# Fused strided attention and MoE on one core: new rules and a new order in the list scheduler, the softmax term as a column, gates kept in PSUM

## The chip, the core and the metric

The kernel runs on one core of a Trainium2 chip as one launch. The metric is the device time of the launch in microseconds; lower is better. The kernel before has a median of 315.19 us over three runs (315.13 to 317.72).

## The reference, cut to what matters

Attention over 8 batches, 8 heads, 576 positions and head size 64 in f32. Heads 0 to 3 see the last 32 positions, heads 4 to 7 every 32nd position. Its output, as 4608 rows of 512, goes to a mixture of 8 experts that picks one expert per row and keeps at most 80 rows of each expert, those with the greatest gate.

```python
mask_local = (rel >= 0) & (rel < stride)
mask_strided = (rel >= 0) & (pos[None, :] % stride == pos[:, None] % stride)
scores = scores - np.max(scores, axis=-1, keepdims=True)
attn = np.exp(scores)
attn = attn / (np.sum(attn, axis=-1, keepdims=True) + 1e-09)
...
probs = np.exp(logits_shift)
probs /= probs.sum(-1, keepdims=True) + 1e-09
gate_w = probs[np.arange(N), expert_idx]
...
keep = np.argpartition(-gw, capacity)[:capacity]
h = np.maximum(x[tok_idx] @ w1[e], 0.0)
out[tok_idx] = gate_w[tok_idx, None] * (h @ w2[e])
```

## The kernel before, in words

The program has three stages.

**Attention**, up to about 213 us of the profiled execution. It is cut into 32 steps j = 4b + 2g + it: batch b, kind of mask g (0 local, 1 strided), half it. For each step PE writes a mask and the scores into PSUM banks (`do_scores`, L503 to L531); DVE takes the maximum (L537) and the difference into an SBUF tile `pb` (L539); ACT makes the exponential in place (L546); DVE sums rows of 64 or 18 (L549), adds 1e-9 (L550) and inverts (L551) into `sm`; POOL multiplies `pb` by `sm` (L553). Two steps later `do_values` transposes `pb` on PE (L581, L612), ACT or DVE copies the result to SBUF, and PE multiplies with v (L598, L641) into `xt`. `do_logits` computes the gate logits of a batch on PE (L657, L660), turns them (L665), and a chain of small DVE instructions (L668 to L699, with an exponential on ACT, L685) makes `gates`. `do_rows` turns `xt` into rows on PE (L732), copies them to an SBUF buffer `xn` (L353, L357) and stores them to `xs` in DRAM (L741). Besides this, POOL moves `vlo` (L461) and `cp` (L411), and 20 chunks of expert weights of 512 KB are loaded (L270) and split into two f16 halves: the high half on POOL or ACT (L280, L278), the low half on DVE (L774).

The order of attention is not written by hand. Each piece of work is an `Op` given to `Plan.add` with a priority, the engine or engines it may run on, a cost in us and what it reads and writes. `Plan.order` is a greedy list scheduler: it advances a clock per engine, picks the earliest operation within `SLACK`, breaks ties by a priority with a random part (`SEED`, `SPREAD`), chooses between ACT and DVE for an operation marked "AV", hands out the 8 PSUM banks, and fills idle PE time with matmuls that nobody reads (`filler`, L370), up to planned time `FILL0` and again past priority `FILL1`. The result is the program order of every engine's queue, SP's included, which issues all loads and stores; each engine runs its queue in that order. Operations marked `lag` (the weight splits) that the plan starts after the last gates go to `late_ops`, and zero fills of `out` that didn't fit go to `pl.dropped`; both are issued after the rows (after L999).

**Router**, about 213 to 241 us. DVE picks 16 candidates per lane (L985 to L998), PE spreads them (`call`, L996), POOL builds `val` (L1019 to L1030), DVE ranks them (L1037 to L1061), PE sums the kept (L1064, L1065), DVE makes one-hot tables (L1075), PE multiplies them (L1078), DVE makes the row numbers `idx` (L1087), and POOL gathers rows (L1092). Rows that the plan doesn't place (`RN` = 14 of the 24 half blocks of the last 4 batches are in it) are turned, copied and stored here by ACT (`rows_left`), through the four buffers of `xns2`, which lie in `vlo` and `ktl`. `warm(n)` (L319) lets PE run n matmuls that nobody reads: 48 behind the rows, 32 behind L1078.

The tiles of the router lie in a pool `rt` that is opened when the pools of attention (`ap`, `am`, `al`) have been closed. It uses their memory, so the first writer of a router tile waits for the last user of the attention tile that lay there.

**Experts**, about 241 to 310 us. 16 halves (w1 or w2 of an expert). PE runs the matmuls (L1149 to L1151, L1171, L1173) while ACT and DVE split the weights of later halves (`wsplit`: L278, L288) and SP reloads the chunk buffers, 8 of them; `xe` is the gathered block of rows turned and split (L1141, L1143, L1144).

## Time and profile before

| | us |
|---|---|
| median of 3 runs | 315.19 |
| profiled execution | 315.96 |
| its span | 314.2 |
| outside the span (315.96 - 314.2) | 1.8 |
| PE busy of the span | 268.0 |
| DVE busy | 244.9 |
| ACT busy | 227.7 |
| POOL busy | 147.4 |
| moved by DMA | 84.24 MB |

Busy times of engines overlap, so they don't add up to the span. Matmuls are pipelined and the profiler draws one until its result is written, so PE's busy time is more than the time it takes from the span. In rows of the trace the first number is the start in us from the span's start, the second how long the engine was in that group; "x12" counts instructions; a bracket at the end gives the idle time ahead of the group and what ended it. "issue" means that the profile shows nothing that the engine waited for.

### The profile page before, as it was taken

The page shows a single profiled execution, that of the slowest core. Times are in us where ns is not written, and L with a number is a line of the kernel's source. Part 1 is how long each engine was busy: PE and PEld are TensorE (multiplying, and loading weights), DVE is VectorE, ACT ScalarE, POOL GpSimd, SP SyncE. Part 2 cuts the span into 40 slices and gives each one's busy share as a digit, 9 for nine tenths or more (in the row PEclk, how much of TensorE's full clock was granted, in tenths as well). Part 3 has the DMA queues.
Part 4 walks back from the last instruction along what each step waited for, and adds up shares of the span by engine and source line. Part 5 has one row for each costly group of instructions (what it writes and reads, how often), then busy time and mean ns, then how long its engine had stood idle before and what let it go on. Part 6 is the DMA issues. An engine that isn't in the chain of part 4 may idle for free. (4 is left out here: it accounts for less than half of the span.)

```text
span 314.2 us, 12290 instructions
## 1 busy us (share of the span) xinstructions
PE 268.0 (85%) x5144; PEld 235.9 (75%) x5144; DVE 244.9 (78%) x489; ACT 227.7 (72%) x446; POOL 147.4 (47%) x170
## 2 busy tenths in 40 slices
PE   7996999899886999889599889896654989999991
PEld 7975977688765987768587758665653989999991
DVE  7594689899997499996778888754484899999980
ACT  1765767789697798779577885775612888999961
POOL 8646458437463556467418518403126252333432
PEclk9999899999999899999799988998955999999997
DMA  8899999999999599997399999869889999999901
GB/s 256 163 269 384 226 265 265 279 293 289 292 287 232 182 261 259 335 277 223 108 249 237 281 246 281 286 170 300 253 266 309 335 371 382 400 385 383 365 28 48
DMA packets 49373, 84.24 MB, mean 268 GB/s; under 512 B 23201, under 2 KB 23201, under 8 KB 49314
## 3 DMA queue, kind: packets, MB, share of 16 engines
q1 hardware_dynamic: 48290, 80.79, 87.4%
q0 software_dynamic: 1024, 2.62, 2.6%
q8 instruction: 42, 0.69, 0.9%
q14 instruction: 17, 0.14, 0.2%
HBM read 63.21 MB, written 20.19 MB: 265 GB/s over the span
## 5 line engine op out<-in xcount | busy, mean ns | idle before, releaser
L553 POOL TENSOR_TENSOR pb<-pb,sm 128x288 f32<-128x288 f32 (+2 forms) x32 | 34.8, 1090 | 66.8 <-DVE sm L551 39.1
L461 POOL TENSOR_SCALAR vlo<-vlo 32x1152 f32<-32x1152 f32 (+1 forms) x32 | 37.8, 1181 | 7.2 <-ACT qt L355 1.8
L774 DVE SCALAR_TENSOR_TENSOR spl<-ring,spl 128x1024 f16<-128x1024 f32 x20 | 27.8, 1398 | 9.3 <-ACT spl L278 9.3
L598 PE MATMUL bank<-ptl,vlo 128*64 128x64 f32 x576 | 24.0, 236 | 9.3 <-issue 8.8
L1149 PE MATMUL hp<-xe,spl 128*128 128x80 f16 x256 | 30.8, 205 | 0.6 <-ACT xe L1143 0.6
L1150 PE MATMUL hp<-xe,spl 128*128 128x80 f16 x256 | 30.7, 205 | 0.7 <-issue 0.3
L1151 PE MATMUL hp<-xe,spl 128*128 128x80 f16 x256 | 30.7, 205 | 0.4 <-issue 0.4
L353 ACT COPY ktl<-bank 64x384 f32<-64x384 f32 (+1 forms) x49 | 26.4, 566 | 5.8 <-DMA xs<-ktl 2.6
L598 PEld LDWEIGHTS bank<-ptl,vlo 128*64 128x64 f32 x576 | 20.8, 147 | 12.7 <-issue 10.8
L1171 PE MATMUL yp<-he,spl 128*128 128x160 f16 x256 | 28.4, 233 | 0.9 <-DVE he L1166 0.9
L1173 PE MATMUL yp<-he,spl 128*128 128x80 f16 x256 | 28.0, 199 | 0.4 <-issue 0.4
L549 DVE TENSOR_REDUCE sm<-pb 128x16 f32<-128x288 f32 (+2 forms) x32 | 22.7, 710 | 7.0 <-ACT pb L546 6.9
L353 ACT COPY ptl<-bank 64x256 f32<-64x256 f32 (+2 forms) x46 | 21.3, 473 | 9.4 <-PE bank L581 5.0
L546 ACT ACTIVATE pb<-pb 128x288 f32<-128x288 f32 (+2 forms) x32 | 18.1, 565 | 13.7 <-DVE pb L539 13.4
L278 ACT ACTIVATE spl<-ring 128x1024 f16<-128x1024 f32 x23 | 23.8, 1059 | 5.7 <-DMA ring<-moe_w 5.7
L288 DVE SCALAR_TENSOR_TENSOR spl<-raw,spl 128x1024 f16<-128x1024 f32 x21 | 26.6, 1288 | 1.0 <-ACT spl L278 1.0
L1150 PEld LDWEIGHTS <-spl 128*128 128x128 f16 x256 | 26.1, 102 | 1.3 <-issue 1.2
L1151 PEld LDWEIGHTS <-spl 128*128 128x128 f16 x256 | 26.1, 102 | 0.9 <-issue 0.9
L1149 PEld LDWEIGHTS <-spl 128*128 128x128 f16 x256 | 26.2, 102 | 0.0
L1173 PEld LDWEIGHTS <-spl 128*128 128x128 f16 x256 | 25.0, 98 | 1.4 <-issue 1.4
L1171 PEld LDWEIGHTS <-spl 128*128 128x128 f16 x256 | 25.1, 98 | 0.9 <-issue 0.9
L628 ACT ACTIVATE pts<-bank,hm 72x288 f32<-72x288 f32 x52 | 21.9, 494 | 3.8 <-DVE pts L622 2.0
(212 smaller groups left out, 776.9 us busy)
## 6 DMA issues: line engine op xcount, KB each, us to landing
ring<-moe_w SPq DMA_DIRECT2D x32, 512.0 KB
raw<-moe_w SPq DMA_DIRECT2D x21, 512.0 KB
raw<-q SPq DMA_DIRECT2D x16, 576.0 KB
out<-kst SPq DMA_DIRECT2D x9, 1024.0 KB
raw<-k SPq DMA_DIRECT2D x15, 576.0 KB
kst<-moe_w SPq DMA_DIRECT2D x11, 512.0 KB
xs<-xn SPq DMA_DIRECT2D x12, 384.0 KB
vs<-v SPq DMA_DIRECT2D x8, 512.0 KB
```

What stands on the lines that cost most here:

```text
L278: nc.scalar.activation(hi, r, AF.Copy, scale=SC)
L288: nc.vector.scalar_tensor_tensor(lo, r, SC, hi, op0=ALU.mult, op1=ALU.subtract)
L353: nc.scalar.copy(o, i)
L461: add(4 * b + m + 0.6 + 0.4 * u, "P", 1.25 if m == 0 else 1.1, lambda e: nc.gpsimd.tensor_scalar(vlo[64 * u:64 * u + 32, t0:t1], vlo[64 * ...
L553: add(pj(j) + E_MUL, "P", 0.2 + 1.7e-3 * nt * nk, lambda e: nc.gpsimd.tensor_tensor(plain(pa, g), plain(pa, g), spread(sm[:, 0:nt], g), op ...
L598: nc.tensor.matmul(o[64 * h:64 * h + 64, :, k0:k0 + 32], vlo[:, 2 * (t0 + c0 + c) + p, h], ptl[:, c0 + c, :, 32 * gg:32 * gg + 32], start= ...
L774: add(pr + 0.2, "V", 1.14, lambda e: nc.vector.scalar_tensor_tensor(lo, r, SC, hi, op0=ALU.mult, op1=ALU.subtract), rd=nm + [("hi", i)], l ...
L1149: nc.tensor.matmul(o, w[:, 0, i:i + P], x[:, 0, c], start=first, stop=False)
L1150: nc.tensor.matmul(o, w[:, 0, i:i + P], x[:, 1, c], start=False, stop=False)
L1151: nc.tensor.matmul(o, w[:, 1, i:i + P], x[:, 0, c], start=False, stop=last)
L1171: nc.tensor.matmul(o.rearrange("p a s -> p (a s)"), w[:, 0, i:i + P], x.rearrange("p a s -> p (a s)"), start=first, stop=False)
L1173: nc.tensor.matmul(o[:, 0], w[:, 1, i:i + P], x[:, 0], start=False, stop=last)
```

## The change

What it does, part by part:

1. **The planner** gets two rules. Operations of DVE and POOL that are marked `port` aren't started while the other engine runs one that is marked too. PE instructions are counted (`ni`), and behind every `NIB` = 252 of them the next can't start before `FETCH` = 5.5 us have passed since the block of instructions before it was entered. Numbers are changed with it: seed, `PEN`, `DLAT`, `E_EXP`, `E_SUM`, `E_O`, `W0`, `LASTN`, `XP0`, `XPS`.
2. **1e-9 as a column**: `pb` becomes wider, with a column of 1e-9 beside every row of 64 (or 18) weights, written once at the start. The sum reads it along with the weights, so the instruction of L550 falls away; in the gates `gex` has a ninth column, and L697 falls away.
3. **Gates**: `lg` and `eq` are no SBUF tiles any more, but columns of the PSUM bank that held the turned logits.
4. **The rows**: `RN` 20 instead of 14 of the last 24 half blocks are in the plan; three of the rest (`XL`) stand ahead of `call`; seven buffers in turn (`xns`, one in `qt`, four as before) instead of four.
5. **The router**: `late_ops` are issued behind the first gather, no longer ahead of the ranking; the one split that stood there goes; 3 splits (`RS`) instead of 1 stand behind the flag, ahead of the first `xe`, and 2 (`NS0`) behind it, as before. `warm` is 48 matmuls behind L1078 in the old numbering, and none behind the rows.
6. The first copies of q and k into `cp` may run on ACT too.

```diff
-    def add(self, prio, eng, cost, fn, rd=(), wr=(), mode=None, take=(), size=0, bg=False, after=(), lag=False, drop=False):
+    def add(self, prio, eng, cost, fn, rd=(), wr=(), mode=None, take=(), size=0, bg=False, after=(), lag=False, drop=False, ni=0, port=False):
...
+                    if o.port:
+                        a, z = port["P" if e == "V" else "V"]
+                        if e in port and a <= t < z:
+                            t = z
...
+            if e == "T":
+                left = NIB - count
+                count += o.ni
+                if count >= NIB and o.ni:
+
+                    x = t + c * left / o.ni
+                    c += max(0.0, entered + FETCH - x)
+                    entered, count = max(x, entered + FETCH), count - NIB
+            if o.port and e in port:
+                port[e] = (t, t + c)
...
+    gex = const.tile([NQ, NC6, E + 1], F32, name="gex")
...
-    pbs = [ap.tile([P, (640, 512, 288, 288)[i]], F32, name=f"pb{i}") for i in range(NPB)]
+    pbs = [ap.tile([P, (650, 520, 304, 304)[i]], F32, name=f"pb{i}") for i in range(NPB)]
...
             for j in range(3):
-                add(l - 2.5, "V", 0.53, lambda e, j=3 * j: nc.vector.tensor_copy(o[:, j:j + 3], i[:, j:j + 3]),
-                    rd=[raw_(l % 3)], wr=[CPS[w][j]])
+                add(l - 2.5, "AV", dict(A=0.45, V=0.53), lambda e, j=3 * j: copy(e, o[:, j:j + 3], i[:, j:j + 3]),
+                    rd=[raw_(l % 3)], wr=[CPS[w][j]], port=True)
...
+    def with_term(pb, g, n):
+        return pb[:, 0:65 * n].rearrange("p (t c) -> p t c", c=65) if g == 0 else \
+            pb.rearrange("p (t c z) -> p t z c", c=19, z=4)
...
         def total(e):
             nc.vector.tensor_reduce(each(sm[:, 0:nt], g), pq, op=ALU.add, axis=AX.X)
-            nc.vector.tensor_scalar(sm[:, 0:nt], sm[:, 0:nt], 1e-9, None, op0=ALU.add)
             nc.vector.reciprocal(sm[:, 0:nt], sm[:, 0:nt])
...
-            nc.vector.tensor_reduce(sg, w["ex"], op=ALU.add, axis=AX.X)
-            nc.vector.tensor_scalar(sg, sg, 1e-9, None, op0=ALU.add)
+            nc.vector.tensor_reduce(sg, gex, op=ALU.add, axis=AX.X)
...
         def lsum(e):
-            w["lg"] = sp.tile([NQ, NC6, E], F32, name="lg")
+            for k_, nm in enumerate(("lg", "eq")):
+                w[nm] = cols(y, 512)[0:NQ, 384 + 64 * k_:432 + 64 * k_].rearrange("p (c e) -> p c e", e=E)
...
+        j = k_ % 2 if b < DEF else (k_ - 3 * DEF) % 7
+        if j < 2:
+            return xns[j], [("xn", j)]
+        return xns2[j - 2], [("xns2", j)] + [[("qt", a) for a in range(3)],
...
+    nc.vector.memset(gex, 1e-9)
+    for t in pbs:
+        nc.vector.memset(t, 1e-9)
...
-    for o in late_ops + pl.dropped:
+    for o in pl.dropped:
         o.fn(o.on)
...
     gather(0)
-    wsplit()
+    for o in late_ops:
+        o.fn(o.on)
     for e in range(1, NX):
         gather(e)
-    flush()
...
-    for _ in range(3 - RS):
+    for _ in range(NS0):
         wsplit()
...
-RN = 14
+RN = 20
 XR = 0
-XL = 4
+XL = 3
 WARM = 44
-WARM_ = [48, 0, 32, 0]
-RS = 1
+WARM_ = [0, 0, 48, 0]
+RS = 3
+NS0 = 2
...
-SEED, SPREAD = 99245, .3
+SEED, SPREAD = 71497, 0.3
...
-LASTB, LASTN = 3, 2
+LASTB, LASTN = 3, 3
...
+NIB, IC0, FETCH = 252, 126, 5.5
```

Three places where the queues differ. The first is DVE from the last gates to the ranking, with the semaphores that each row waits for (`g` is the turned gates, `cvi` or `cv` and `ci` the candidates, `pos` the first tile of the ranking). Before:

```order
L699 TENSOR_TENSOR gates<-eq,sg 96x48 [waits DVE_49]
L904 COPY g_116<-bank_150 128x96 [waits PE_49]
L985 MAX cvi<-g_116 128x8 [waits DVE_49]
L986 MATCH_REPLACE qs<-cvi,g_116 128x288 [waits DVE_49]
L987 MAX cvi<-qs 128x8 [waits DVE_49]
L990 TENSOR_TENSOR wgt<-cvi,segm 128x256 [waits DVE_49]
L997 MAX_INDEX cvi<-cvi,g_116 128x8
L998 MAX_INDEX cvi<-cvi,qs 128x8
L774 SCALAR_TENSOR_TENSOR spl_129<-ring_122,spl_129 128x1024 [waits DMAHW0_49,Activation_49]
L1037 TENSOR_SCALAR pos<-cvi 128x16 [waits DVE_49]
L1039 TENSOR_SCALAR scr,rank<-call,cvi 128x256 [waits PE_49]
```

Now:

```order
L737 TENSOR_TENSOR gates<-bank_152,sg 96x48 [waits DVE_49]
L944 COPY g_117<-bank_152 128x96 [waits PE_49]
L1026 MAX cv<-g_117 128x8 [waits DVE_49]
L1027 MATCH_REPLACE qs<-cv,g_117 128x288 [waits DVE_49]
L1028 MAX cv<-qs 128x8 [waits DVE_49]
L1031 TENSOR_TENSOR wgt<-cv,segm 128x256 [waits DVE_49]
L1038 MAX_INDEX ci<-cv,g_117 128x8
L1039 MAX_INDEX ci<-cv,qs 128x8
L1078 TENSOR_SCALAR pos<-cv 128x16 [waits DMAHW0_49,DMAHW1_49,DVE_49,Activation_49]
L1080 TENSOR_SCALAR scr,rank<-call,cv 128x256 [waits PE_49]
```

The split of a weight chunk (L774) between the candidates and the ranking is gone. `pos` now waits for an ACT copy and two stores as well: in the program these are the copy into the row buffer that lies in `qt` and the two stores from that buffer, because `pos` lies where `qt` lay. The first instruction of POOL's `pieces` waits for the same.

The second place is SP's queue from the first stores of the last rows to the first loads of the expert stage (`xs<-` are row stores, `out<-kst` are zero fills of 1 MB). Before, and below it now:

```order
L741 DMA xs<-ktl 96x1024
L741 DMA xs<-vlo 96x1024 x2
L741 DMA xs<-ktl 96x1024 x2
L270 DMA ring_122<-moe_w 128x1024
L794 DMA out<-kst 256x1x1024
L270 DMA kst<-moe_w 128x1024
L270 DMA kst<-moe_w 128x2x512
L270 DMA raw<-moe_w 128x2x512 x3
```

```order
L295 DMA ring_123<-moe_w 128x1024
L834 DMA out<-kst 256x1x1024 x2
L780 DMA xs<-vlo 96x1024
L295 DMA ring_124<-moe_w 128x1024
L780 DMA xs<-ktl 96x1024
L780 DMA xs<-xn_181 96x1024
L780 DMA xs<-xn_182 96x1024
L780 DMA xs<-qt 96x1024
L780 DMA xs<-vlo 96x1024
L780 DMA xs<-ktl 96x1024
L780 DMA xs<-vlo 96x1024 x2
L295 DMA raw<-moe_w 128x2x512 x3
```

All zero fills and weight loads of the plan now stand ahead of the last row stores, the last stores go to five buffers in turn instead of two, and the loads into `raw` are the first behind them, where a weight load and a zero fill were.

The third place is DVE from the flag to the first block of rows (`ovfb` is what PE multiplies to sum the flag, `fls` and `fli` the flag). Before, and below it now:

```order
L1114 CAST ovfb<-ovf 128x2
L1117 TENSOR_REDUCE fls<-small 1x1
L1119 CAST fli<-fls 1x1
L288 SCALAR_TENSOR_TENSOR spl_3610<-ring_122,spl_3610 128x1024
L1144 SCALAR_TENSOR_TENSOR xe<-xp,xe 128x320
L288 SCALAR_TENSOR_TENSOR spl_3610<-raw,spl_3610 128x1024
```

```order
L1155 CAST ovfb<-ovf 128x2
L1158 TENSOR_REDUCE fls<-small 1x1
L1160 CAST fli<-fls 1x1
L313 SCALAR_TENSOR_TENSOR spl_3424<-ring_123,spl_3424 128x1024
L313 SCALAR_TENSOR_TENSOR spl_3424<-ring_124,spl_3424 128x1024
L313 SCALAR_TENSOR_TENSOR spl_3424<-raw,spl_3424 128x1024
L1185 SCALAR_TENSOR_TENSOR xe<-xp,xe 128x320
```

Three splits now stand between the flag and the first block of rows (`xe`), where one stood; before, another one (of `ring_121`) stood some rows further up, right behind `idx` (L1087), and now none does.

More of the change, by code (lines that the diff above doesn't have):

```diff
@@ L92, in order @@
         dma, mode, fills = 0.0, None, []
+        port = dict(V=(0.0, 0.0), P=(0.0, 0.0))
+        count, entered = IC0, 0.0
         rng = random.Random(SEED)
@@ L137, in order @@
                     f.mode, f.cost, f.deps, f.take, f.size, f.lag = 128, m * C_FILL, [], (), 0, False
+                    f.port, f.ni = False, 2 * m
+                    count += f.ni
+                    if count >= NIB:
+                        entered, count = f.start, count % NIB
                     fills.append(f)
@@ L344, in moe_attention @@
     xns2 = [t[0:NQ, 1024 * j:1024 * j + 1024].rearrange("p (x f) -> p x f", x=2)
-            for t in (vlo.rearrange("p t h d -> p (t h d)"), ktl.rearrange("p h u s -> p (h u s)")) for j in range(2)]
+            for t, m in ((qtl.rearrange("p h s -> p (h s)"), 1), (vlo.rearrange("p t h d -> p (t h d)"), 2),
+                         (ktl.rearrange("p h u s -> p (h u s)"), 2)) for j in range(m)]
     def cols(x, n):
@@ L434, in do_transposes @@
             add(pr, "T", C_TR * 3, fill, rd=[CPS[w][j3]] if g == 0 else nm, wr=[x], take=[x], mode=128,
-                after=[((("qt", j3), ("qs", j3))[g]) if w == 0 else ((("ktl", u, j3), ("kst", u, j3))[g]) for u in range(len(dvs))])
+                after=[((("qt", j3), ("qs", j3))[g]) if w == 0 else ((("ktl", u, j3), ("kst", u, j3))[g]) for u in range(len(dvs))], ni=6)
             for u, d in enumerate(dvs):
@@ L462, in do_overlap @@
             vlo[64 * u:64 * u + 32, t0:t1], vlo[64 * u + 32:64 * u + 64, t0 - 1:t1 - 1], 1.0, 0.0,
-            op0=ALU.mult, op1=ALU.add), rd=[("vlo", u, m), ("vlo", u, 0)], wr=[("vlq", u, m)])
+            op0=ALU.mult, op1=ALU.add), rd=[("vlo", u, m), ("vlo", u, 0)], wr=[("vlq", u, m)], port=True)
     def rows_of(t, g):
@@ L510, in do_scores @@
                                                                          [("qs", a) for a in range(3)] + KST + ["mstr", "kstz"]),
-                wr=[x], take=[x], mode=128, after=[("p", j % NPB, bk)])
+                wr=[x], take=[x], mode=128, after=[("p", j % NPB, bk)], ni=4 if g == 0 and t == 0 else 2)
             if g == 0:
@@ L521, in mm @@
                                                  tile_position=(0, 32 * gg))
-                add(pj(j), "T", 0.112 * n, mm, rd=[("qt", a) for a in range(3)] + KTL + ["ktlz"], wr=[x], mode=32)
+                add(pj(j), "T", 0.112 * n, mm, rd=[("qt", a) for a in range(3)] + KTL + ["ktlz"], wr=[x], mode=32, ni=8 * n)
                 t += n // 2
@@ L532, in mm @@
                                                  start=False, stop=(rr == 1 and z == 3), tile_position=(0, 32 * h))
[L533 removed]
+                    add(pj(j), "T", 0.57, mm, rd=[("qs", a) for a in range(3)] + KST + ["kstz"], wr=[x], mode=32,
+                        ni=64)
             sv = lambda x=x, n=n: rows_of(cols(x, n * nk), g)
[L535 removed]
+            pv_ = by_row(weights(pb, g, o, n), g)
             su = lambda x=x, n=n: plain(cols(x, n * nk), g)
@@ L575, in do_values @@
             t0 = TL[it][0]
+            pn = [[("ptl", a, u) for a in ((a,) if it == 0 else (0, 1))] for a in range(2) for u in range(2)]
             for a, (c0, c1) in enumerate(TG[it]):
@@ L580, in fill @@
                     for c in range(n):
-                        nc.tensor.transpose(cols(x, 512)[:, P * c:P * c + P], pb[:, P * (c0 + c):P * (c0 + c) + P], ident)
+                        nc.tensor.transpose(cols(x, 512)[:, P * c:P * c + P], pb[:, 130 * (c0 + c) + 1:130 * (c0 + c) + 129], ident)
                 add(pj(j) + E_PT, "T", C_TR * n, fill, rd=PN, wr=[x], take=[x], mode=128,
-                    after=[("ptl", a, u) for u in range(2)])
+                    after=pn[2 * a] + pn[2 * a + 1], ni=2 * n)
                 for u in range(2):
@@ L599, in mm @@
                                                  ptl[:, c0 + c, :, 32 * gg:32 * gg + 32], start=True, stop=True)
-                add(pj(j) + 2, "T", 0.25 * n, mm, rd=[("ptl", a, u) for u in range(2)] + [("vlq", u, it) for u in range(2)] +
-                    [("vlo", u, it) for u in range(2)] + ["vloz"], wr=[x], take=[x], mode=64, after=nm)
+                add(pj(j) + 2, "T", 0.25 * n, mm, rd=pn[2 * a] + pn[2 * a + 1] + [("vlq", u, it) for u in range(2)] +
+                    [("vlo", u, it) for u in range(2)] + ["vloz"], wr=[x], take=[x], mode=64, after=nm, ni=16 * n)
                 add(pj(j) + 2 + E_O, "AV", c_copy(P * n), lambda e, x=x, c0=c0, c1=c1, n=n: copy(
@@ L611, in fill @@
                 for a in range(4):
-                    nc.tensor.transpose(t[0:72, a], pb[:, 72 * a:72 * a + 72], ident)
+                    nc.tensor.transpose(t[0:72, a], pb[:, 76 * a:76 * a + 72], ident)
             add(pj(j) + E_PT, "T", C_TR * 4, fill, rd=PN, wr=[x], take=[x], mode=128,
-                after=[("pts", z) for z in (0, 2)])
+                after=[("pts", z) for z in (0, 2)], ni=8)
             def tv(x):
@@ L755, in do_rows @@
         xn, nm = xn_of(b, hf)
-        add(pr, "T", C_TR * 4, lambda e: fill(cols(x, 512)), rd=xt_of(b, part)[1], wr=[x], take=[x], mode=128)
+        add(pr, "T", C_TR * 4, lambda e: fill(cols(x, 512)), rd=xt_of(b, part)[1], wr=[x], take=[x], mode=128, ni=8)
         add(pr + E_EV, "AV", c_copy(512), lambda e: ev(e, cols(x, 512), xn),
```

81 lines of the change are left out of this document (39 added, 42 removed).

## Prediction

> **What bounds the kernel now.** I read the slices of the span and the windows view first, to find which engine limits which stretch; then the waits of PE, since PE is busiest in the longest stretch; then the timelines of the stretch between.
>
> ```profile
> 8.00:213.00 205.00, 182.49 (x3585) 153.95 (x3582) 163.10 (x353) 157.56 (x340) 105.92 (x103) 0.97 0.94 255
> 245.00:306.00 61.00, 58.36 (x1278) 56.97 (x1275) 58.41 (x63) 55.66 (x84) 21.90 (x23) 1.00 0.91 334
> 102.10:152.40 50.30, 44.71 (x885) 37.96 (x885) 40.22 (x88) 40.38 (x88) 27.53 (x25) 0.97 0.89 255
> 101.60:104.90 3.30, 2.80 (x33) 2.68 (x34) 1.65 (x6) 1.20 (x3) 2.75 (x3) 0.50 0.87 286
> 152.80:156.10 3.30, 3.30 (x25) 3.18 (x21) 1.61 (x5) 1.98 (x4) 1.94 (x3) 0.50 0.11 25
> ```
>
> (After the window: its length, then busy us and count of PE, weight loads, DVE, ACT, POOL; last the granted clock, the DMA share and GB/s.) Attention is a PE stage: 182.49 of 205 us, DVE 163.10, with DMA close behind at a share of 0.94. The expert stage has PE and DVE level, 58.36 and 58.41 of 61.
>
> ```profile
> PE bank L598 <- issue: 8.8, 7, 3.2
> PE bank L612 <- POOL pb L553: 2.8, 3, 1.1
> PE bank L519 <- issue: 1.2, 1, 1.2
> PE bank L641 <- issue: 1.2, 1, 1.2
> PE bank L531 <- issue: 0.4, 2, 0.2
> PE bank L432 <- DVE pb L539: 0.6, 2, 0.4
> ```
>
> Of PE's waits in attention (total, times, longest) the largest ended on nothing that the profile shows: 8.8 + 1.2 + 1.2 + 0.4 = 11.6 us of "issue". For DVE it waits 0.6.
>
> ```profile
> 99.03 0.57 PE L598 MATMUL bank<-ptl,vlo 128*64 128x64 f32 x12
> 102.10 1.76 PE L598 MATMUL bank<-ptl,vlo 128*64 128x64 f32 x28 [2.50 <-issue]
> 152.45 0.89 PE L598 MATMUL bank<-ptl,vlo 128*64 128x64 f32 x15 [3.16 <-issue]
> q8 instruction: 42, 0.69, 0.9%
> ```
>
> Between the two stalls lie 885 = 7 x 126 + 3 matmuls, each of two PE instructions. So the stalls recur at a fixed count, 252 instructions, and a DMA queue brings the instructions (0.69 MB / 42 = 16 KB a packet). A block of short matmuls ends before its successor is there. Behind a stall of this length the granted clock is 0.50 for 3.30 us (two windows above).
>
> From the last copy of gates (`g`, which I call T0 = 212.76) to PE at full pace:
>
> ```profile
> 212.76 0.26 DVE L904 COPY g<-bank 128x96 f32<-128x96 f32 x1 [0.46 <-PE bank L791]
> 215.44 0.45 DVE L998 FIND_INDEX8 cvi<-cvi,qs 128x8 uint32<-128x288 f32 x1
> 224.26 1.23 DVE L774 SCALAR_TENSOR_TENSOR spl<-ring,spl 128x1024 f16<-128x1024 f32 x1 [8.37 <-ACT spl L278]
> 225.41 0.17 DVE L1037 TENSOR_SCALAR pos<-cvi 128x16 f32<-128x16 f32 x1
> 233.10 0.17 DVE L1087 TENSOR_REDUCE idx<-tab 80x8 int32<-80x16 f32 x1 [0.81 <-PE tab L1078]
> 236.61 0.15 DVE L1117 TENSOR_REDUCE fls<-small 1x1 f32<-1x2 f32 x1 [0.80 <-PE small L1115]
> 236.87 1.23 DVE L288 SCALAR_TENSOR_TENSOR spl<-ring,spl 128x1024 f16<-128x1024 f32 x1
> 239.94 0.77 PE L1141 MATMUL xp<-ident,xg 80*128 80x80 f32 x4 [3.37 <-DMA xg<-xs,idx]
> 241.81 0.23 PE L1150 MATMUL hp<-xe,spl 128*128 128x80 f16 x1 [0.30 <-DVE xe L1144]
> ```
>
> DVE stands 8.37 us before the ranking (`pos`), behind one split whose ACT half was late: ACT had row copies ahead of it, and those waited for stores from their buffers (the 2.63 in a row further down). The stretch is 241.81 - 212.76 = 29.05 us long.
>
> **The change part by part, in attention (what it does to T0).**
>
> *Instruction blocks.* I took the printed order of PE in both kernels, gave every matmul the mean spacing that its form has in the trace, and summed each 126. Before, the blocks fall short of 5.5 us by 10.9 in total, where the profile has 11.6: the model holds. The new order falls short by 5.4: -5.5. Ends: -7 (its short blocks stretched by waits) and 0 (the stalls don't follow this rule).
>
> *Half clock.* Each long stall costs about 3.3 x 0.5 = 1.7 us more. Summed in the same way, the shortest block before is 2.7 us and now 3.8, so stalls of 2.5 us and more shouldn't come again; I take one of the two as gone: -1.7 (-3.4 to 0).
>
> *Twenty more row transposes* (five half blocks of four) stand ahead of T0 in PE's order:
>
> ```profile
> 213.07 2.00 PE L732 MATMUL bank<-ident,cp 128*96 128x128 f32 x16 [0.35 <-DVE g L904]
> 210.59 1.50 PE L370 MATMUL bank<-identb 128*128 128x128 bf16 x24
> ```
>
> At 2.00/16 = 0.125 us that is +2.5. 75 fewer fillers (0.06 each, second row, 4.7 us) stand in the order, but they lie where PE would wait: 0, and -4.7 would be the end below.
>
> *The gates' tail.* In the chain that gives T0 there is now no split:
>
> ```profile
> 209.49 1.22 DVE L774 SCALAR_TENSOR_TENSOR spl<-ring,spl 128x1024 f16<-128x1024 f32 x1
> 210.62 0.20 DVE L688 TENSOR_TENSOR eq<-lg,m 96x48 f32<-96x48 f32 x1
> 211.68 0.17 DVE L697 TENSOR_SCALAR sg<-sg 96x6 f32<-96x6 f32 x1
> ```
>
> The split held L688 for 1.1, L697 took 0.2. Against that stand the PSUM operands of the gates: the copy of 96 columns from PSUM above took 0.26 where SBUF instructions of 48 take 0.20, so up to 0.06 for each of some six: -1.0 (-1.3 to -0.9).
>
> *The 1e-9 column.* It removes 32 + 8 instructions of DVE:
>
> ```profile
> L550 DVE TENSOR_SCALAR sm<-sm 128x16 f32<-128x16 f32 (+2 forms) x32 | 11.6, 364 | 1.1
> L697 DVE TENSOR_SCALAR sg<-sg 96x6 f32<-96x6 f32 x8 | 2.9, 362 | 0.3
> ```
>
> 14.5 us of DVE (364 ns is a mean over 171 to 1005). I value it at 0: PE's own work covers it, since PE waits 0.6 us for DVE in the whole stage; were that cover gone, the end below is -0.6. New at the start are memsets of 1778 columns on DVE, by the splits (1024 columns, 1.22 us) 1.6 to 2.1, partly under the first loads: +0.5 (0 to +1).
>
> *Port rule.* Reordered DVE and POOL work that PE doesn't wait for longer than 2.8 us: inside the terms above.
>
> *DMA.* Two row stores, a weight chunk and a zero fill more go out ahead of T0: 2 x 0.39 + 0.52 + 1.05 = 2.4 MB, at 255 GB/s 9.3 us. The idle share, 6% of 205 = 12.3 us, takes it nearly all: +1 (0 to +3).
>
> *Moved work.* The last weight split (1.2 us of DVE, about 1 us of ACT) and the zero fill that stood behind T0 stand ahead of it. DVE has 205 - 163.1 = 42 us without work there and ACT 47, and PE hardly waits for either: 0. The same holds for three early copies of `cp` that may go to ACT, which is idle then. What the split frees behind T0 is counted below.
>
> Sum: -5.5 - 1.7 + 2.5 - 1.0 + 0.5 + 1 = **-4.2**. The ends add up to -14.4 and +5.6, but they can't all come together, since stalls, fillers and waits share the same idle time of PE; I keep -9 to +3.
>
> A rule of the Trainium skill speaks against the first term: "Runtime: NRT & Kernel Launch", Instruction fetch mechanics, says that crossing a 16 KiB boundary costs one DMA tail-bump that is mostly hidden. The trace disagrees, with 11.6 us of issue stalls at that period. By the page the blocks would be worth nothing, nor would the half clock behind them, T0 would move by 2.5 - 1.0 + 0.5 = +2.0, and the first rival below would hold.
>
> **The stretch behind T0.** *Ranking.* The split is gone, and `pos` now waits for the row copy into `qt` and its store:
>
> ```profile
> 211.15 0.44 SPq L741 DMA_DIRECT2D xs<-ktl  x1
> 217.19 1.07 ACT L353 COPY ktl<-bank 96x512 f32<-96x512 f32 x2 [2.63 <-DMA xs<-ktl]
> 218.28 0.32 SPq L741 DMA_DIRECT2D xs<-ktl  x1
> 221.23 2.05 ACT L353 COPY ktl<-bank 96x512 f32<-96x512 f32 x4
> ```
>
> A store behind other transfers landed 217.19 - 211.15 = 6.0 us after issue, one in a thin queue 221.23 - 218.28 = 2.95 or less. The second `qt` copy stands about 1 us behind T0, so `pos` starts at T0 + 4.6; the ends are T0 + 3.1 (candidates done, 215.89) and T0 + 7.2. From `pos` to the end of `idx` took 233.27 - 225.41 = 7.86.
>
> ```profile
> 216.06 0.23 POOL L1019 CAST pieces<-cvi 128x16 bf16<-128x16 f32 x1 [15.63 <-DVE cvi L998]
> 219.91 1.28 POOL L1030 TENSOR_TENSOR val<-pieces,esel 128x640 bf16<-128x640 bf16 x1
> 231.61 1.46 PE L1078 MATMUL tab<-val,oh 128*80 128x40 bf16 x16 [1.19 <-DVE oh L1075]
> ```
>
> POOL's `val` takes 221.19 - 216.06 = 5.1 and runs beside the ranking now; L1078 needs it 231.61 - 225.41 = 6.2 behind `pos`, so it is hidden, with +0.3 (0 to 1.5) for two engines on one port. `idx`: T0 + 12.8 instead of T0 + 20.5.
>
> *Flag and splits.* 48 fillers stand ahead of the flag's matmul where 32 stood:
>
> ```profile
> 222.03 2.84 PE L319 MATMUL bank<-identb 128*128 128x128 bf16 x48
> 232.90 3.58 PE L319 MATMUL bank<-identb 128*128 128x128 bf16 x32
> ```
>
> At the pace of the second row 48 x 3.58/32 = 5.4 (by the first 2.8). They start 0.4 ahead of the end of `idx`: T0 + 17.8; flag to DVE 236.87 - 236.41 = 0.46: T0 + 18.3; three splits of 1.2: T0 + 21.8; L1144 to full PE pace 0.5: **T0 + 22.3**. The gather is next: issue 0.3 behind `idx`, landing 239.94 - 233.58 = 6.4, then 241.81 - 239.94 = 1.9: T0 + 21.4, a microsecond earlier. So 29.05 - 22.3 = **-6.7**; with `pos` at T0 + 7.2 and the contention -4.0, with the early `pos` and fast fillers -8.9.
>
> **Expert stage**: the same instructions on two level engines, 0; the loads have one chunk less, so a gain of up to 1.2 isn't excluded.
>
> **Sum**: profiled 315.96 (span 314.2 + 1.8) - 4.2 - 6.7 = 305.06. The median lies 0.8 below the profiled execution: **304.3 us**.
>
> **The rivals.** *Attention is not faster*: the stalls come again at other places, or other waits fill them; T0 moves by +2.0 (2.5 - 1.0 + 0.5; without faster PE the transfers keep their time; ends 0 and +3), and only the router gains: 315.19 + 2.0 - 6.7 = **310.5** (308.5 to 311.5). For it: the new order's sum hangs on where the count begins; shifted by some 40 matmuls it falls short by 13.3. Against it: the model met 11.6 with 10.9 at the phase that the trace has.
>
> *The router gain is eaten too*: `pos` hangs behind two 1 MB zero fills and row stores in SP's queue, so that `idx` comes as late as before, and T0 is as in the rival above: **314** (312.1 to 316). For it: a store took 6.0 us here already; against it: it would have to take some 12.
>
> *DMA becomes the bound of attention* (the other side): the 9.3 us of added transfers find no idle time, nothing is gained from the blocks because PE waits for loads instead, T0 is 9.3 late, the router gives back 6.7 to 4.0: **317.8 to 320.5**. It decides when less than 2 of the 12.3 idle us can be used. For it: the share is 0.94 already; against it: in the window 102.10 to 152.40 the share is 0.89, so there is room.
>
> **How the numbers follow.** Forecast 0.64, attention not faster 0.21, router eaten 0.09, DMA 0.06. A measurement of this kernel tells about 1% (3.2 us) from no change. The first two lie over 1% below 315.19: faster 0.85; the third within: 0.09; the last above: 0.06. The forecast's own ends are 300 (T0 earlier by 8.5, a little inside its end) and 308.5 (T0 as before); to leave out no more than 2 in 10 the range takes in the first rival: 300.0 to 311.5.
>
> **What would show it.** Right: issue stalls of PE of about 5 to 6 us in attention; T0 near 208.5; no wait of DVE over 3 us ahead of `pos`; `idx` 12 to 13 us behind T0; PE in the experts' matmuls without a break from T0 + 22; the expert stage 61 us as before. Wrong: issue stalls near 11 (first rival); `pos` waiting over 5 us for a DMA (second); PE waiting for loads into `raw` and `vlo`, or for row stores, with the DMA share at 1.0 (third). If `xe` waits for DMA rather than for splits, the last step fails.

## The result, and the profile after

The changed kernel: median **301.33 us** over four runs (297.42 to 304.67), before 316.46 over four. The ratio is **0.944, interval 0.931 to 0.956**; it compares the undisturbed executions of both, so it lies under the ratio of the medians (0.952). Faster by over 1%, as forecast, but the ratio times 315.19 is 297.5, below the range's low end of 300. (The plain median, 301.33, lies inside the range.) The profiled execution took 297.42 (span 295.7). A later set of four gave 305.23 (300.96 to 307.13) against 318.15, ratio 0.964 (0.947 to 0.981).

The windows view of the profile after, cut just behind T0 (197.02) and at PE's full pace (224.3); columns as in the prediction:

```profile
8.00:197.20 189.20, 173.79 (x3544) 148.87 (x3541) 150.33 (x324) 151.37 (x329) 107.92 (x106) 0.99 1.01 283
197.20:224.30 27.10, 9.62 (x93) 8.46 (x92) 16.10 (x55) 9.77 (x16) 9.74 (x19) 0.71 0.88 289
224.30:295.70 71.40, 63.86 (x1341) 62.10 (x1340) 59.10 (x66) 56.82 (x87) 25.02 (x25) 0.95 0.80 289
```

T0 came 15.7 us earlier (forecast 4.2). The stretch behind it took 27.3 us instead of 29.05 (forecast 22.3), the rest 71.4 instead of 72.4. Besides DVE's busy time (163.10 to 150.33), two columns moved in attention: the granted clock from 0.97 to 0.99, and the DMA share from 0.94 to 1.01. By the share, DMA has hardly any idle time left; it is no hard limit, though, since the kernel before stands at 1.06 from 160 to 200 us.

All of PE's issue stalls in attention, first of this execution (3.8 us in all, before 11.6), then of a second execution of the same kernel (9.7 us, T0 204.11):

```profile
PE bank L639 <- issue: 1.7, 3, 0.9
PE bank L396 <- issue: 1.5, 1, 1.5
PE bank L559 <- issue: 0.6, 1, 0.6
```

```profile
PE bank L706 <- issue: 3.7, 1, 3.7
PE bank L639 <- issue: 2.9, 4, 1.6
PE bank L458 <- issue: 1.5, 1, 1.5
PE bank L571 <- issue: 1.0, 1, 1.0
PE bank L682 <- issue: 0.6, 1, 0.6
```

One program, two executions, 5.9 us of stalls and 7.1 us of T0 apart; the second lies outside what was expected of it (T0 197 to 202, stalls of 4 to 7). A T0 from one profile is therefore good to some 4 or 5 us to either side, and below it is read beside the stalls of its own execution and the median of the runs.

DVE behind T0, in the profile after:

```profile
197.02 0.26 DVE L944 COPY g<-bank 128x96 f32<-128x96 f32 x1 [0.61 <-PE bank L831]
206.39 0.17 DVE L1078 TENSOR_SCALAR pos<-cv 128x16 f32<-128x16 f32 x1 [6.23 <-DMA xs<-qt]
210.36 1.23 DVE L1095 TENSOR_SCALAR pos<-thr 128x4 f32<-128x4 f32 x1
215.47 0.17 DVE L1128 TENSOR_REDUCE idx<-tab 80x8 int32<-80x16 f32 x1 [0.81 <-PE tab L1119]
219.90 0.15 DVE L1158 TENSOR_REDUCE fls<-small 1x1 f32<-1x2 f32 x1 [2.77 <-PE small L1156]
223.78 0.48 DVE L1185 SCALAR_TENSOR_TENSOR xe<-xp,xe 128x320 f16<-128x320 f32 x1
```

Where DVE stood 8.37 us for ACT's half of a split, it now stands 6.23 us for a row store. `idx` is done 18.6 us behind T0, not 12.8. SP's queue tells why:

```profile
184.16 2.12 SPq L834 DMA_DIRECT2D out<-kst  x2
190.36 0.32 SPq L780 DMA_DIRECT2D xs<-vlo  x1
193.93 1.66 SPq L780 DMA_DIRECT2D xs<-ktl  x1
196.18 4.60 SPq L780 DMA_DIRECT2D xs<-xn  x2
200.87 1.26 SPq L780 DMA_DIRECT2D xs<-qt  x1
```

Two zero fills of 1 MB go out at 184 us, and four row stores stand between them and the store from `qt`, which is issued at 200.87 and releases `pos` 5.5 us later. SP needed 4.60 us to issue the two stores from `xn`; with the zero fills out of the way (zeros_late below) it needed 1.29.

### The profile page after: what moved, and what is told of

Read it like the earlier page. It is cut to its first block, busy times and chain, and to the rows that moved or that the text cites. A ratio compares the mean times of both kernels' runs of the same rounds, so it can differ in the third digit from the quotient of the medians.

```text
span 295.7 us, 12041 instructions
## 1 busy us (share of the span) xinstructions
PE 253.5 (86%) x5037; PEld 225.7 (76%) x5037; DVE 231.4 (78%) x461; ACT 220.2 (74%) x433; POOL 148.0 (50%) x172
## 5 line engine op out<-in xcount | busy, mean ns | idle before, releaser
L487 POOL TENSOR_SCALAR vlo<-vlo 32x1152 f32<-32x1152 f32 (+1 forms) x32 | 39.5, 1234 | 11.5 <-DMA vlo<-v 5.5
L1191 PE MATMUL hp<-xe,spl 128*128 128x80 f16 x256 | 31.3, 207 | 1.5 <-DVE xe L1185 1.3
L1190 PE MATMUL hp<-xe,spl 128*128 128x80 f16 x256 | 31.4, 207 | 0.6 <-ACT xe L1184 0.6
L1192 PE MATMUL hp<-xe,spl 128*128 128x80 f16 x256 | 31.3, 207 | 0.0
L1212 PE MATMUL yp<-he,spl 128*128 128x160 f16 x256 | 28.2, 233 | 0.0
L589 DVE TENSOR_REDUCE sm<-pb 128x16 f32<-128x304 f32 (+2 forms) x32 | 23.5, 736 | 4.8 <-ACT pb L586 4.6
L639 PE MATMUL bank<-ptl,vlo 128*64 128x64 f32 x576 | 21.6, 225 | 5.2 <-issue 1.7
L639 PEld LDWEIGHTS bank<-ptl,vlo 128*64 128x64 f32 x576 | 19.1, 138 | 8.6 <-issue 2.4
L571 PEld LDWEIGHTS bank<-kst,qs 128*18 128x18 f32 x1024 | 18.9, 118 | 5.3 <-issue 1.1
L571 PE MATMUL bank<-kst,qs 128*18 128x36 f32 x1024 | 22.3, 246 | 0.6 <-ACT kst L379 0.6
L379 ACT COPY ktl<-bank 64x384 f32<-64x384 f32 (+1 forms) x37 | 20.4, 560 | 2.4 <-PE bank L771 1.0
L303 ACT ACTIVATE spl<-ring 128x1024 f16<-128x1024 f32 x21 | 22.0, 1057 | 0.0
```

The lines of the kernel that those rows point to most:

```text
L487: add(4 * b + m + 0.6 + 0.4 * u, "P", 1.25 if m == 0 else 1.1, lambda e: nc.gpsimd.tensor_scalar(vlo[64 * u:64 * u + 32, t0:t1], vlo[64 * ...
L571: nc.tensor.matmul(so[32 * h:32 * h + 18, rr, :, z], qts[:, h, r::16], kst[:, :, h, r::16], start=False, stop=(rr == 1 and z == 3), tile_p ...
L589: nc.vector.tensor_reduce(each(sm[:, 0:nt], g), pq, op=ALU.add, axis=AX.X)
L639: nc.tensor.matmul(o[64 * h:64 * h + 64, :, k0:k0 + 32], vlo[:, 2 * (t0 + c0 + c) + p, h], ptl[:, c0 + c, :, 32 * gg:32 * gg + 32], start= ...
L1190: nc.tensor.matmul(o, w[:, 0, i:i + P], x[:, 0, c], start=first, stop=False)
L1191: nc.tensor.matmul(o, w[:, 0, i:i + P], x[:, 1, c], start=False, stop=False)
```

## The experiments

T0, the stalls and the stretches are each of one profiled execution; medians and intervals are of the timed runs. "Stalls" are PE's issue waits from 8 us to T0, "clock" is the mean granted one there, "PE" the time from T0 to full pace (the start of the second matmul of the first product), "rest" from there to the end.

| kernel | median | ratio to before (interval) | T0 | stalls | clock | PE | rest |
|---|---|---|---|---|---|---|---|
| before | 316.46 | 1 | 212.76 | 11.6 | 0.97 | 29.05 | 72.43 |
| changed | 301.33 | 0.944 (0.931-0.956) | 197.02 | 3.8 | 0.99 | 27.29 | 71.39 |
| phase_after | 308.23 | 0.973 (0.961-0.985) | 204.87 | 11.0 | 0.98 | 29.82 | 73.12 |
| phase_before | 312.58 | 0.988 (0.973-1.003) | 208.45 | 12.7 | 0.98 | 30.40 | 71.37 |
| e1_back | 308.90 | 0.983 (0.972-0.994) | 205.37 | 2.7 | 0.99 | 27.30 | 72.28 |
| qt_am | 303.22 | 0.961 (0.946-0.975) | 200.21 | 6.6 | 0.98 | 28.19 | 71.81 |
| after_again | 305.23 | 0.964 (0.947-0.981) | 204.11 | 9.7 | 0.98 | 28.06 | 71.79 |
| before_no550 | 315.71 | 1.001 (0.995-1.007) | 212.67 | 15.6 | 0.96 | 31.81 | 71.56 |
| before_thin | 318.21 | 1.013 (1.000-1.025) | 212.56 | 12.8 | 0.97 | 31.44 | 72.46 |
| zeros_late | 300.63 | 0.955 (0.942-0.968) | 200.32 | 7.7 | 1.00 | 25.27 | 73.02 |
| zeros_am | 306.56 | 0.973 (0.964-0.983) | 203.21 | 7.3 | 0.99 | 21.93 | 77.80 |
| plan_nofetch | 307.02 | 0.977 (0.968-0.985) | 203.39 | 6.8 | 0.97 | 27.52 | 75.67 |
| plan_noport | 299.51 | 0.951 (0.940-0.962) | 207.94 | 15.5 | 0.97 | 27.67 | 72.76 |
| plan_neither | 317.37 | 1.005 (0.993-1.018) | 209.96 | 11.7 | 0.96 | 28.94 | 72.38 |
| seed1_fetch | 308.04 | 0.982 (0.974-0.991) | 213.00 | 12.0 | 0.97 | 22.30 | 71.42 |
| seed1_none | 306.65 | 0.977 (0.964-0.989) | 210.82 | 9.9 | 0.96 | 24.04 | 73.82 |
| seed3_fetch | 305.62 | 0.975 (0.960-0.989) | 204.14 | 10.9 | 0.98 | 27.38 | 71.93 |
| seed3_none | 307.99 | 0.981 (0.961-1.000) | 207.61 | 10.5 | 0.97 | 26.18 | 72.10 |
| noport_again | 300.04 | 0.950 (0.942-0.958) | 197.55 | 3.6 | 1.00 | 27.37 | 71.39 |
| noport_zeros | 302.24 | 0.955 (0.947-0.963) | 198.39 | 6.8 | 0.99 | 28.66 | 72.60 |

### Do the instruction blocks set the stalls? (phase_after, phase_before)

```diff
-    warm(WARM)
+    t = bank()
+    for _ in range(WARM + 60):
+        nc.tensor.matmul(t[:, 0:2], identb, identb[:, 0:2], start=True, stop=True)
```

> The changed kernel with its first 44 matmuls that nobody reads replaced by 104 narrow ones (2 columns instead of 128), so that every border of 126 matmuls falls 60 matmuls earlier in the program; nothing else. Theory A (PE stalls where 126 matmuls take less than 5.5 us): summed as in the prediction, the blocks fall short by 13.3 us at this phase and by 5.4 in the changed kernel; issue stalls of PE in attention go from 3.8 to 10 to 12 us, with two to three more half-clock windows, and T0 from 197.0 to 205 to 209. Theory B (the stalls went because of other parts of the change: port rule, less DVE work, transfers): T0 stays within 2 us of 197.

> The kernel before with the same edit of its first 44 matmuls. Theory A: the blocks fall short by 3.5 us at this phase instead of 10.9; issue stalls go from 11.6 to about 4, half-clock windows in attention from 4 to 1 or 2, and T0 from 212.8 to 202 to 206. Theory B: T0 stays within 2 us of 212.8.

The changed kernel with its borders moved:

```profile
PE bank L571 <- issue: 3.9, 4, 1.4
PE bank L639 <- issue: 3.8, 2, 3.2
PE bank L682 <- issue: 1.9, 2, 1.2
PE bank L559 <- issue: 1.4, 1, 1.4
```

The kernel before with its borders moved:

```profile
PE bank L531 <- issue: 5.6, 2, 4.2
PE bank L598 <- issue: 2.2, 4, 0.9
PE bank L732 <- issue: 2.1, 1, 2.1
PE bank L432 <- issue: 1.7, 1, 1.7
PE bank L519 <- issue: 1.1, 1, 1.1
```

The first came out as theory A had it: 11.0 us of stalls, T0 204.87, and a median 5.0 over qt_am's, which has the same attention and ran beside it. That doesn't prove it: the changed kernel with its borders unmoved also reached 9.7 us and 204.11 (after_again), and the intervals of phase_after and qt_am overlap. The second missed theory A: 12.7 us where the count gave about 4, though T0 was 4.3 earlier with less half clock (its ratio, 0.988, doesn't exclude 1). The stalls did move with the count (matmuls counted from the start of the program): the largest of phase_before (4.2 us) comes ahead of its matmul 855, that of the kernel before (3.2) ahead of 2623, and 855 and 2623 leave 99 and 103 over a multiple of 126. It holds for every kernel of the table: each of the 77 issue stalls of 1 us or more ahead of T0, in all 20 profiles, comes 97 to 106 matmuls over a multiple of 126. So the count tells **where** PE can stall. How long it stalls there is not "5.5 us less the block's own time". Eight blocks of under 3 us were each followed by a stall of 1.6 to 3.7 us, but 29 of the 77 stalls follow a block that took more than 5.5 us by itself: the 4.2 us above a block of 6.26, the 3.7 of after_again one of 6.81.

### Is the shorter DVE work worth anything? (e1_back, before_no550)

```diff
+            nc.vector.tensor_scalar(sm[:, 0:nt], sm[:, 0:nt], 1e-9, None, op0=ALU.add)
             nc.vector.reciprocal(sm[:, 0:nt], sm[:, 0:nt])
...
+            nc.vector.tensor_scalar(sg, sg, 1e-9, None, op0=ALU.add)
             nc.vector.reciprocal(sg, sg)
```

> The changed kernel with the 32 + 8 small DVE instructions put back ahead of the reciprocals (they add 1e-9 a second time, which is all that they change). The planned order is the same. Theory A (DVE has room, the 14.5 us of DVE that the column saves are worth nothing): T0 within 1.5 us of 197.0. Theory B (the saved DVE work is where the gain beyond the forecast came from): T0 later by 5 us or more.

> The kernel before without the 32 + 8 DVE instructions that add 1e-9 (the term is left out, nothing stands in its place); the order is the same otherwise. Putting them back into the changed kernel made T0 8.4 us later. Theory A (DVE is a bound of attention in any order): T0 5 to 9 us earlier than 212.8, with less waiting of PE for POOL's pb. Theory B (the old order leaves DVE room, and only the new one, planned with the shorter DVE work, needs it): T0 within 2 us of 212.8.

The window of attention in e1_back, and PE's three longest waits for DVE there:

```profile
8.00:205.40 197.40, 173.93 (x3529) 146.80 (x3528) 163.48 (x364) 151.69 (x329) 106.30 (x106) 0.99 0.98 271
```

```profile
PE bank L458 <- DVE gates L739: 1.6, 2, 0.8
...
PE bank L683 <- DVE g L941: 1.2, 1, 1.2
PE bank L773 <- DVE pts L664: 1.1, 1, 1.1
```

DVE works 163.48 us where the changed kernel's does 150.33, and T0 is 8.4 us later, in an execution with only 2.7 us of issue stalls; the median is 5.7 over qt_am's in the same set, and the two kernels' runs don't overlap (306.66 to 310.95 against 300.42 to 306.43). Taking an execution's own issue stalls off its T0 makes it plainer: 202.7 in e1_back, 192.6 to 195.9 in the six profiles with the changed kernel's attention (changed, phase_after, qt_am, after_again, zeros_late, zeros_am). PE's other waits add up to 20.2 us in e1_back and to 9.8 to 12.8 in those six. So in the new order DVE's 14 us are worth 5 to 8. (e1_back keeps the order that was planned without these instructions. No run planned the changed kernel anew with them kept, so what the column is worth to the planner stays open.) In the old order they are worth nothing (0.995 to 1.007). PE's waits in before_no550, and below them a row of the kernel before:

```profile
PE bank L597 <- issue: 11.0, 5, 3.7
PE bank L531 <- issue: 3.8, 2, 2.5
PE bank L611 <- POOL pb L552: 1.3, 2, 1.0
...
PE bank L580 <- POOL pb L552: 0.5, 1, 0.5
```

```profile
PE bank L581 <- POOL pb L553: 2.3, 1, 2.3
```

The waits for POOL's `pb` fell from 2.8 + 2.3 to 1.3 + 0.5, and the issue stalls rose from 11.6 to 15.6, as if the wait removed had come back as another one. That is a reading and not shown, since the stalls of one program differ by as much between two executions.

### Are the fillers free? (before_thin)

```diff
     def filler(i, m):
         for _ in range(m):
-            nc.tensor.matmul(banks[i][:, 0:P], identb, identb, start=True, stop=True)
+            nc.tensor.matmul(banks[i][:, 0:2], identb, identb[:, 0:2], start=True, stop=True)
```

> The kernel before with its 143 filler matmuls of the plan cut from 128 columns to 2, their number kept, so that the instruction blocks stay where they are. Theory A (fillers stand on PE's path): 143 x 0.04 = 5 to 6 us off T0. Theory B (they lie where PE would wait anyway, as the prediction held): T0 within 1.5 us of 212.8, and waits of PE longer by 5 us.

Theory B: T0 212.56. PE is busy 176.97 us instead of 182.49, and waits come to light that weren't in the view before, these among them:

```profile
PE bank L506 <- DVE sm L550: 1.4, 1, 1.4
PE bank L791 <- DVE gates L699: 1.1, 1, 1.1
PE bank L598 <- POOL cp L411: 1.1, 1, 1.1
```

So a row "waits 0.6 us for DVE" was not all of PE's waiting for DVE: with the 0.4 us ahead of the last gates it is 1.0 in the kernel before, and with thin fillers 2.7. The planner had put fillers into the rest, and a filler counts as work. The rest is 1.7 us, though, and not 5 to 8.

### What holds the ranking and the first gather? (qt_am, zeros_late, zeros_am)

```diff
-    qtl = ap.tile([P, 2, S], F32, name="qt")
+    qtl = am.tile([P, 2, S], F32, name="qt")
```

> The changed kernel with the tile qt in the pool am instead of ap; the order is the same and pos and pieces no longer wait for a row copy and two stores. Theory A (the 6.2 us wait of pos for the store from qt ate the router's gain): pos starts 3.2 us behind T0 instead of 9.4; the gather then waits for the last row store, 14.5 us behind T0, instead of being issued at 18.9; PE at full pace near T0 + 22.5 instead of T0 + 27.3, 4 to 5 us gained in all. Theory B (the last row stores, or the weight splits, end the stretch no earlier): less than 1.5 us gained.

`pos` started 3.2 us behind T0 and `idx` came at + 12.0, as theory A had it; PE's full pace still came at + 28.2, as theory B had it. POOL's first gather:

```profile
219.07 1.22 POOL L1133 DMA_INDIRECT xg<-xs,idx  x1 [10.45 <-DMA raw<-moe_w]
```

POOL stood ready 10 us. The load named there isn't what the gather reads: it must wait for every row store, and the last of these landed 17.7 us behind T0, with the store queue as full as before. Next the two zero fills were moved behind the gathers, from a small tile of zeros (the first diff; in zeros_am qt_am's edit is added, and they stand behind the first five splits):

```diff
-        if o.start > final.start and o.lag:
+        if o in fills[-2:]:
+            zeros.append(o)
+        elif o.start > final.start and o.lag:
...
     for e in range(1, NX):
         gather(e)
+    for j in range(len(zeros)):
+        nc.sync.dma_start(outv[8 - j].rearrange("p r (a f) -> p (r a) f", a=4), z2.unsqueeze(1).broadcast_to([64, 16, 256]))
```

> The changed kernel with its last two zero fills (2 MB) taken out of SP's queue ahead of the last row stores and put behind the gathers (from a small tile of zeros). Theory A (behind T0 the end is set by the row stores, which stand in the DMA queue behind 2 MB of zeros, some 5 to 6 us at 350 to 400 GB/s): the last row store lands 8 to 10 us behind T0 instead of 14.5, pos starts at T0 + 4 instead of + 9.4, the gather is issued at T0 + 12 to 13 instead of + 18.9, PE at full pace at T0 + 22 to 23 instead of + 27.3; T0 the same within 2 us; the expert stage no longer than 72.5. Theory B (the queue is full whatever stands in it, or weight loads take the place): less than 2 us gained behind T0, or the 2 MB come back as a longer expert stage.

> The changed kernel with qt in the pool am (pos no longer waits for its store) and the last two zero fills behind the five first splits of the expert stage in SP's queue, so that they can't go out ahead of the gathers. In the run with the zeros right behind the gathers SP put them out 4 us ahead of the first gather, whose landing then took 8.4 us. Theory A (the row stores and then the gather in a crowded queue set the stretch): last row store 11 us behind T0, idx at + 12.5, gather issued at + 13, landing 6 to 7 later, PE at full pace at T0 + 21 to 22 where the changed kernel has 27 to 28; expert stage up to 1.5 us longer, median some 4 to 5 us under the changed kernel's. Theory B (flag, fillers and splits are last next): PE at T0 + 24 or later.

zeros_late won 2 to 3 us behind T0, and 1.2 to 1.6 came back in the rest; its median is 4.6 under after_again's, but the intervals overlap (0.942 to 0.968 against 0.947 to 0.981). zeros_am reached the forecast's place, 21.9 us behind T0:

```profile
225.14 0.22 PE L1197 MATMUL hp<-xe,spl 128*128 128x80 f16 x1 [0.77 <-DVE xe L1191]
```

and lost it all again. Its windows behind that point:

```profile
225.20:240.00 14.80, 14.77 (x315) 14.69 (x315) 13.07 (x16) 11.36 (x17) 3.64 (x5) 0.87 0.99 312
240.00:260.00 20.00, 14.97 (x290) 14.42 (x290) 14.32 (x16) 13.93 (x21) 7.23 (x7) 0.91 1.03 368
260.00:302.90 42.90, 35.15 (x741) 33.79 (x738) 32.44 (x36) 31.80 (x50) 14.49 (x15) 0.98 0.68 255
```

and ACT's first late split there:

```profile
245.03 1.06 ACT L303 ACTIVATE spl<-raw 128x1024 f16<-128x1024 f32 x1 [6.00 <-DMA raw<-moe_w]
```

From 240 to 260 DMA is at 1.03 and PE is busy for 14.97 of 20 us: ACT waits 6.00 us for a weight load that SP issued behind the zeros, and PE for the split. The rest takes 77.8 us instead of 71.4. The transfers are owed, and here moving them only moved the wait. (seed1_fetch, below, had them done in time.)

### The rules, or the order that came out? (plan_nofetch, plan_noport, plan_neither, two other seeds)

```diff
-NIB, IC0, FETCH = 252, 126, 5.5
+NIB, IC0, FETCH = 252, 126, 0.0
```

```diff
-        o.lag, o.drop, o.ni, o.port = lag or bg, drop, ni, port
+        o.lag, o.drop, o.ni, o.port = lag or bg, drop, ni, False
```

The first diff is plan_nofetch, the second plan_noport, both together plan_neither. The seed kernels have the second and SEED 1 or 3, "none" also the first.

> The changed kernel with FETCH at 0 in the planner, so that it plans without the instruction blocks; same seed, another order. By the count of the prediction its blocks fall short by 8.8 us where the changed kernel's fall short by 5.4. Theory A (the rule is worth what it avoids): T0 3 to 6 us later than the 197 to 204 of the changed kernel, issue stalls above 10. Theory B (issue stalls move by several us between executions whatever the plan): times within 1% of the changed kernel's.

> The changed kernel with the port rule off in the planner; same seed, another order, whose blocks fall short by 5.0 us. Theory A (keeping marked DVE and POOL work apart is worth much): the splits of DVE and POOL last longer on average, DVE is busier by 5 us or more, T0 3 us or more later. Theory B (worth little): T0 and the median within 1% of the changed kernel's.

> The changed kernel with both rules off in the planner, which leaves the new costs, the column, the gates in PSUM and the rows; blocks short by 9.3 us. Theory A (the gain of attention comes from the shorter DVE work planned anew): T0 within 4 us of the changed kernel's 197 to 204, far under 212.8. Theory B (it comes from the two rules): T0 at 208 or later.

> The changed kernel planned with seed 1 instead of 71497 and the port rule off, FETCH 5.5 kept. Its blocks fall short by 10.1 us by the count of the prediction. Theory A (the rule makes any order faster): T0 under 205 and a median near the 299.5 to 303.6 of the chosen seed. Theory B (what counts is how far the blocks of the order that came out fall short, and the chosen seed has one of 5): T0 208 to 213, median 308 to 316. Theory C (the order's other waits decide): no relation to the shortage.

> The same with FETCH 0, seed 1: short by 9.5 us. Theory A: T0 6 us or more later than with the rule. Theory B: within 2 us of it, 308 to 316. Theory C: no relation.

> Seed 3, port rule off, FETCH 5.5: short by 8.8 us. Theory A: median near 299.5 to 303.6. Theory B: 306 to 313. Theory C: no relation.

> Seed 3, port rule off, FETCH 0: short by 5.9 us, less than with the rule. Theory A: slower than with the rule by 6 us or more. Theory B: faster than with the rule, by some 3 to 5 us, near 302 to 307. Theory C: no relation.

After the first three the block rule looked like everything: with the chosen seed and no port rule 299.5 with it, 317.4 without. One sign spoke against it: plan_nofetch, planned without the rule, has 6.8 us of stalls, where theory A had over 10 and the changed kernel has 3.8 and 9.7. The other seeds took the rest away: 308.0 with the rule and 306.7 without, 305.6 and 308.0. Nor does the shortage order them: the order short by 5.9 us (seed3_none) is no faster than those short by 8.8 to 10.1, and only the two at 5.0 and 5.4 stand apart. Theory A fell, theory B isn't borne out, theory C fits best. What the four seed kernels share is a gain without the port rule, and in two of them without either rule: ratios of 0.975 to 0.982, some 6 to 8 us of 315 (the interval of seed3_none just reaches 1). The chosen seed's two orders planned with the block rule lie lower (0.944 to 0.964; the intervals overlap in part), and plan_neither shows that one unlucky order can lose everything. How seed 71497 was found isn't known here; if it was the best of many, its lead over seeds 1 and 3 comes from the search and not from a rule.

seed1_fetch also answers the question of the section before. DVE there:

```profile
217.98 0.17 DVE L1078 TENSOR_SCALAR pos<-cv 128x16 f32<-128x16 f32 x1 [1.06 <-DMA xs<-qt]
```

`pos` starts 5.0 us behind T0 and PE is at full pace at + 22.3, as the prediction had it for the changed kernel, and the rest takes 71.42 as before. Its order issued the last zero fill 23 us ahead of T0 and not 13, in an attention that ended only at 213.00. So the short stretch behind T0 need not cost the expert stage when the transfers are done before it begins. T0 came 16 us later here, though, so no run shows the early T0 and the short stretch together.

### The better version? (noport_again, noport_zeros)

The edits are plan_noport's alone, and with that of zeros_late.

> The order with the port rule off once more (four executions gave 297.7, 297.9, 301.1 and 310.2, the profiled one the slowest). Theory A (this order is a little faster than the changed kernel's, and the 310.2 had a bad draw of instruction stalls): median 298 to 302, T0 199 to 202 in a usual execution with issue stalls of 5 to 9. Theory B (the orders are equal, 303 to 306).

> The same order with its last two zero fills behind the first gathers. In the changed kernel's order that brought PE to full pace 2 to 3 us earlier behind T0 and gave 1.2 to 1.6 back in the expert stage. Theory A (row stores behind zeros set the router): 1 to 3 us under the run without. Theory B (the transfers are owed anyway): the same within 1 us or slower.

Without the port rule ten executions of the order gave 297.7 to 310.2, half of them below 300; eight of the changed kernel gave 297.4 to 307.1, one below 300. The order is no slower that shows, at 0.950 (0.942 to 0.958), so the port rule earns nothing that shows. Its two profiles, again of one program:

```profile
PE bank L571 <- issue: 9.4, 3, 3.3
PE bank L559 <- issue: 2.3, 3, 1.3
PE bank L458 <- issue: 1.9, 1, 1.9
PE bank L396 <- issue: 1.3, 1, 1.3
PE bank L639 <- issue: 0.6, 1, 0.6
```

```profile
PE bank L458 <- issue: 1.7, 1, 1.7
PE bank L396 <- issue: 1.2, 1, 1.2
PE bank L571 <- issue: 0.5, 2, 0.3
PE bank L559 <- issue: 0.2, 1, 0.2
```

15.5 and 3.6 us of stalls, T0 207.94 and 197.55, times 310.17 and 298.03; less their stalls the two T0 are 192.4 and 194.0. Moving the zero fills gained nothing here (302.24 beside 300.04).

## Why the prediction was right and wrong, step by step

**What bounds it.** Attention was PE's, and its stalls fell on the instruction count: right, and seen again where the borders were moved. The 0.94 of DMA deserved more weight: the changed kernel stands at 1.01, and row stores set its stretch behind T0.

**Instruction blocks, -5.5.** The profiled execution lost 7.8 us of stalls, the second 1.9, and the three kernels with the same attention and borders (qt_am, zeros_late, zeros_am) 5.0, 3.9 and 4.3. The mean, 4.6, is near the term, but by luck, since its working failed: "the model holds" rested on one order at one phase in one execution. At another phase it gave 3.5 for 12.7, one program gave 3.6 and 15.5, and over a third of the long stalls follow blocks that by the model can't stall. The Trainium skill's "Runtime: NRT & Kernel Launch", Instruction fetch mechanics, has the crossing "mostly hidden". Single stalls of up to 4.8 us at these counts (seed1_fetch), and sums of 2.7 to 15.6 us over attention, speak against that as a price.

**Half clock, -1.7.** Mis-sized. In attention the clock stood at 0.50 for four stretches of 3.4 us before, for one in the changed kernel and for 6.8 us in one piece in its second execution. By half of these times that is some 5.1 and 3.4 us of matmul time at full pace (an estimate). I had in mind only the two stretches behind stalls of 2.5 us and more; the other two don't follow such a stall. Nor is the rule exact: in before_no550 a stall of 2.6 us (up to 55.89) has the clock at 1.00 behind it.

**1e-9 column, 0.** This is the step that failed. The price was right for the old order (before_no550: no gain) and wrong for a new one: there the same work is worth 5 to 8 us. I took "PE's own work covers it" from the old order's view, PE's 0.6 us of waits for DVE, and carried it over to an order in which that cover is gone. Fillers hid some of the waiting, but 1.7 us of it only (2.7 against 1.0 in before_thin), so they alone don't explain the miss. The fillers' own price, 0, is borne out: thin, they save nothing. That 75 fewer were planned may have been a sign that the planned waits had shrunk; I put 4.7 us of it only into the bound, and no run tests this.

**Router, -6.7.** 1.8 and 1.0 measured. The failed step is "`pos` starts at T0 + 4.6": the bounds reached to + 7.2, and it was + 9.4, since the store was neither early (issued at + 3.9) nor in a thin queue (5.5 us to release `pos`). That is the second rival's mechanism; it took 4.9 and 5.7 of the 6.7 us. (Two of my sums here don't hold: `pos` at + 7.2 and the contention together cost 2.6 + 1.2, so the term's upper end is -2.9 and not -4.0; and the second rival's own words give 315.19 + 2.0 = 317.2 and not 314.) Yet with that wait gone (qt_am) the last row stores took its place, and with the zeros gone (zeros_am) PE came to full pace at + 21.9, forecast + 22.3, and paid in the expert stage. So DMA wasn't late by one bad wait; the bytes were owed when attention ended early, and with a later end (seed1_fetch, T0 213.00) the forecast's + 22.3 came without that price. A smaller miss: for DVE working beside POOL I took 0.3 us, and one instruction alone lost 1.1.

**Expert stage, 0:** 71.4 and 71.8 after 72.4: right.

**The sum.** -4.2 - 6.7 became -15.7 - 1.8 - 1.0 in the profiled execution. The second one, T0 204.11, PE + 28.06 and rest 71.79, gives -8.7 - 1.0 - 0.6. The total of the forecast lay between the two, with its parts swapped: too little in attention and too much behind it. Of the -15.7, 7.8 are stalls and 8.0 are not, where the forecast had -5.5 and, for all other terms, +1.3. The 5 to 8 us of DVE and the 3.4 us of half clock beyond its term would fill the 9.3 us between (an estimate: T0 less its stalls is 195.8 to 201.2 in the three profiles of the old order with all of its instructions, so the 8.0 is uncertain by some 5). What stays open is how much of attention's gain each other part brings: each change of the plan is another order, and orders of equal parts differ by 10 us.
